# Linear attention in transposed 64x64 float32 tiles, with sums of squares and factors made by products with selectors

## The chip, the cores and the metric

The kernel runs on one core of a Trainium2 chip. The metric is the device time of one execution in microseconds (us). Abbreviations in the rows: PE is TensorE (matrix products), PEld its weight loads, DVE is VectorE, ACT is ScalarE, POOL is GpSimd, SP the engine that issues most transfers.

## What is computed

Three stages follow one another, all in float32, for 8 batches, 8 heads, 576 tokens and 64 features a head. Only the first is touched.

```
kv  = einsum('bhsd,bhde'): k^T v of each head          # 64 x 64 state, over all 576 tokens
out = q @ kv                                           # per head
out = out / sqrt(mean(out*out over the head) + 1e-6) * g_norm
x   = out, heads side by side                          # [8, 576, 512]
# second stage: xk, xr = blends of each token with the one before it
r = sigmoid(xr @ w_r);  v = relu(xk @ w_k)**2 @ w_v;   x = r * v
# third stage: attention of 4 experts, the best 2 per token, summed
```

The state has no causal mask: it sums over all tokens before any head's output can start.

## The kernel before

**Phase 1** makes the first two stages, batch by batch. Large products run as three passes in a rounded format (`mm3`: high part times high part, low times high, high times low; lines 59 to 61), each pass 128x128 weights against 288 columns, half of a batch's 576 tokens. One half needs 4 r groups of 12 passes (`r_group`; batch 0 does those of both halves first), 8 k groups of 12 (`k_group`) and 4 v groups of 24 (`v_group`); a batch is 480 passes. `acc`, the accumulator, has 4 banks.

The 20 weight tiles come as double words and are converted on the chip (`wconv`, `words`): five VectorE steps each on 128x512 (lines 140 to 151), and then for the 12 tiles of w_r and w_k three products, for the 8 of w_v two GpSimd operations (lines 179 and 180).

**`front(b)`** is the linear attention of one batch. It takes 5 chunks of tokens, 128 four times and 64. The state: 8 products of 64x64 per chunk into the bank `kvp` (line 217), copied by ScalarE into `kvbd`, which holds two heads on a block diagonal of 128x128. Heads: a chunk of q is the weight and `kvbd` moves, 4 products to `po`, tokens on partitions (line 240). ScalarE squares (244) and copies (245), VectorE reduces over each head (246). The factor 1/sqrt is made on 128 x 40 numbers (`rsqrt`, 249 to 269: for batch 0 ScalarE's root and a reciprocal in two parts with one Newton step, else a bit trick and three steps). The scaling is a GpSimd product (VectorE for batch 0), `scaled`; then `turned` transposes each chunk by four products with the identity (283) and ScalarE writes `xT`, features on partitions, with g. `mix` blends neighbours of `xT` and splits the blend in a high and a low part (327 to 334).

**Order.** A driver at the end of `phase1` runs one step of the generator `front(b+1)` after each group of batch b; within that, every engine's order is set by a scheduler that simulates the engines and uses the buffers as they come free. K(0,1) below is the first `k_group` of batch 0's second half. VectorE's part of a k group that makes the low part `kl` stands behind a GpSimd product (361, 362). Phase 2, from 566 us, makes the third stage.

The functions in question, with the line numbers of the rows:

## Time and profile before

| | |
|---|---|
| median of 3 runs | 1039.02 us (1038.98 to 1040.86) |
| profiled execution | 1040.45 us, span of the core 1038.7 |
| TensorE busy | 1007.7 us, 97% |
| VectorE, ScalarE, GpSimd busy | 540.1 (52%), 535.2 (52%), 306.1 (29%) |

Busy time is summed over the whole span and says nothing of a single stage; a matrix product in the rows overlaps the next, so starts rather than durations are to be subtracted. A float32 product leaves two records on TensorE. "x16" is the number of records merged in a row; what stands in brackets is idle time before it and what ended that.

### The profile page before, as it was taken

Reading aid. Unit: us, or ns where it says so; the run is one execution under the profiler, and the core shown is the slowest. Engines: PE = TensorE matmul, PEld = TensorE weight load, DVE = VectorE, ACT = ScalarE, POOL = GpSimd, SP = SyncE. Lnnn points to the kernel's source line nnn. Section 1 sums busy time; section 2 is a strip of 40 time slices with the busy share of each in tenths; the row PEclk is TensorE's granted clock in tenths of the full one; section 3 lists DMA queues with packets and bytes.
Section 4 is the critical chain, followed back from the end, with each engine's and each line's share of the span. In section 5 each row is a group of like instructions: output and inputs, shape, how many; then the busy total and the mean of one; then the engine's idle time right before and its main releaser. Section 6 shows DMA issues by size and latency. Waiting matters only on the chain.

```text
span 1038.7 us, 20745 instructions
## 1 busy us (share of the span) xinstructions
PE 1007.7 (97%) x7968; PEld 925.9 (89%) x7968; DVE 540.1 (52%) x1524; ACT 535.2 (52%) x1381; POOL 306.1 (29%) x459
## 2 busy tenths in 40 slices
PE   6797899999999999999999999999999999999998
PEld 4587799999999999999999999888888888888876
DVE  4989934344533434444354531367464746556563
ACT  4975544544644554465375533356453736454544
POOL 0017622213212212212123113165251616243331
PEclk9998999999999999999999999999999999999999
DMA  8972200001041041040101201210111202020102
GB/s 278 314 256 84 83 25 24 23 24 54 2 130 54 2 151 34 15 146 25 44 26 45 84 24 25 66 46 27 66 47 47 80 13 93 1 93 27 46 13 80
DMA packets 46259, 70.56 MB, mean 68 GB/s; under 512 B 8016, under 2 KB 25936, under 8 KB 46160
## 3 DMA queue, kind: packets, MB, share of 16 engines
q1 hardware_dynamic: 37712, 59.79, 17.7%
q10 hardware_dynamic: 8448, 9.44, 3.0%
q8 instruction: 63, 1.03, 0.4%
q14 instruction: 36, 0.29, 0.1%
HBM read 50.34 MB, written 18.87 MB: 67 GB/s over the span
## 4 chain that ended last, share of the span: by engine, by line
PE 89%; DVE 6%; DMA 3%; issue 1%; ACT 1%; SPq 0%; POOL 0%; ACTq 0%; DVEq 0%; POOLq 0%
PE acc L59 23%; PE acc L60 22%; PE acc L61 22%; PE acc L668 5%; PE pt L640 5%; PE s L592 4%; PE po L240 3%; PE kvp L217 2%; PE pt L283 1%; PE s L583 1%; DMA raw<-in_w_r 1%; DVE wvl L151 1%; DVE cvt L144 1%; DVE xm L328 1%; DMA qt<-in_qT 1%
## 5 line engine op out<-in xcount | busy, mean ns | idle before, releaser
L361 POOL TENSOR_TENSOR ksq<-rl 128x288 f32<-128x288 f32 x128 | 91.2, 712 | 322.0 <-ACT rl L358 314.6
L59 PE MATMUL acc<-xh,wkh 128*128 128x288 f32 x512 | 154.4, 302 | 2.8 <-ACT rl L358 2.8
L60 PE MATMUL acc<-xl,wkh 128*128 128x288 f32 x512 | 152.9, 299 | 2.5 <-DVE xl L334 2.5
L60 PE MATMUL acc<-kl,wvh 128*128 128x288 f32 x512 | 150.8, 297 | 3.6 <-DVE kl L362 3.5
L61 PE MATMUL acc<-xh,wkl 128*128 128x288 f32 x512 | 152.9, 299 | 0.0
L61 PE MATMUL acc<-kh,wvl 128*128 128x288 f32 x512 | 150.2, 296 | 0.0
L59 PE MATMUL acc<-kh,wvh 128*128 128x288 f32 x512 | 146.8, 296 | 0.0
L604 ACT ACTIVATE pr<-pr,nm 128x256 f32<-128x256 f32 (+4 forms) x144 | 83.4, 580 | 76.0 <-DVE nm L564 73.5
L362 DVE TENSOR_TENSOR kl<-ksq,kh 128x288 fp32r<-128x288 f32 x128 | 60.8, 475 | 90.8 <-POOL ksq L361 89.0
L621 POOL TENSOR_SCALAR pr<-pr,rc,wg 128x512 f32<-128x512 f32 (+3 forms) x128 | 76.4, 609 | 100.5 <-DVE wg L557 57.5
L59 PEld LDWEIGHTS acc<-xh,wkh 128*128 128x128 f32 x512 | 97.5, 191 | 4.9 <-ACT rl L358 3.0
L60 PEld LDWEIGHTS acc<-kl,wvh 128*128 128x128 f32 x512 | 96.5, 189 | 4.5 <-DVE kl L362 4.5
L60 PEld LDWEIGHTS acc<-xl,wkh 128*128 128x128 f32 x512 | 97.6, 191 | 2.7 <-DVE xl L334 2.7
L61 PEld LDWEIGHTS acc<-xh,wkl 128*128 128x128 f32 x512 | 97.6, 191 | 0.0
L61 PEld LDWEIGHTS acc<-kh,wvl 128*128 128x128 f32 x512 | 96.6, 189 | 0.0
L59 PEld LDWEIGHTS acc<-kh,wvh 128*128 128x128 f32 x512 | 95.3, 189 | 0.1
L347 ACT ACTIVATE sg<-acc 128x288 f32<-128x288 f32 x64 | 26.1, 408 | 122.1 <-PE acc L61 122.1
L331 DVE TENSOR_TENSOR xl<-xm,xh 128x288 fp32r<-128x288 f32 x96 | 45.0, 508 | 69.9 <-ACT xh L329 69.7
L59 PE MATMUL acc<-x2h,wqh 128*128 128x256 f32 (+1 forms) x256 | 78.9, 308 | 0.7 <-DVE sg L374 0.4
L59 PE MATMUL acc<-xh,wrh 128*128 128x288 f32 x256 | 78.2, 306 | 0.0
L358 ACT ACTIVATE rl<-acc 128x288 f32<-128x288 f32 x128 | 52.1, 409 | 50.4 <-PE acc L61 49.0
L374 DVE TENSOR_TENSOR sg<-acc,sg 128x288 f32<-128x288 f32 x64 | 29.0, 456 | 93.0 <-PE acc L61 92.5
(154 smaller groups left out, 2576.2 us busy)
## 6 DMA issues: line engine op xcount, KB each, us to landing
x2d<-sg SPq DMA_DIRECT2D x16, 576.0 KB, 3.4
out<-ob SPq DMA_DIRECT2D x28, 288.0 KB, 2.1
kt<-in_k SPq DMA_DIRECT2D x31, 256.0 KB, 3.4
vt<-in_v SPq DMA_DIRECT2D x31, 256.0 KB, 3.5
qt<-in_qT SPq DMA_DIRECT2D x31, 256.0 KB, 2.8
x2in<-x2d ACTq DMA_DIRECT2D x8, 640.0 KB, 4.4
raw<-in_w_k SPq DMA_DIRECT2D x8, 512.0 KB, 6.5
raw<-in_w_v SPq DMA_DIRECT2D x8, 512.0 KB, 3.8
```

The source lines that it names most:

```text
L59: nc.tensor.matmul(ps, wh(i), xh(i), start=(i == 0), stop=False)
L60: nc.tensor.matmul(ps, wh(i), xl(i), start=False, stop=False)
L61: nc.tensor.matmul(ps, wl(i), xh(i), start=False, stop=(i == n - 1))
L331: nc.vector.tensor_sub(xl[:, p - 1, :], xp, xh[:, p - 1, :].bitcast(F32))
L358: nc.scalar.activation(rl, acc, AF.Relu)
L361: nc.gpsimd.tensor_mul(sq, rl, rl)
L362: late.append(lambda: nc.vector.tensor_sub(kl[:, m, :], sq, kh[:, m, :].bitcast(F32)))
L592: nc.tensor.matmul(sts[b, p, j][:, r, :L], qs[h, x, t0:t0 + n], ks[h, y, :L], start=(i == 0), stop=(i == 2))
L604: nc.scalar.activation(pr[:, :L], pr[:, :L], AF.Exp, bias=nm, scale=-1.0, accum_out=sms[b, p, j][:, e2:e2 + 1])
L621: nc.gpsimd.tensor_scalar(pr[:, :L], pr[:, :L], rc[:, r:r + 1], wg, op0=ALU.mult, op1=ALU.mult)
L640: nc.tensor.transpose(pt[:rows, (i - i0) * P:(i - i0 + 1) * P], pr[:, i * P:i * P + rows], ident)
L668: nc.tensor.matmul(y[r * D:(r + 1) * D, a:w], vs[:kn, i, e * D:(e + 1) * D], pT[:kn, r, i, a:w], start=(i == 0), stop=(i == idx[-1]), skip ...
```

## The change

The state keeps its form (8 products of 64x64 per chunk), in chunks of 128, 128, 128, 112 and 80 tokens, and goes as a plain 64-row copy per head into `kv`; `kvbd` goes. Heads are made transposed: the state is the weight, 64x64, on the four tiles of the array that two row halves and two column halves make, and q, laid out by the host with features on partitions, moves in 288 columns, so that the output comes out in the layout of `xT`. ScalarE squares it and copies it into `xT` unscaled. The mean over a head is a product of the squares with `sels` (ones over 64, 128x32) into `sm`, which shares the bank of `kvp`. The factors are made on [64 or 128] x 288 numbers, split in a high and a low row, and spread over the features by products with `selb` (ones), and VectorE multiplies `xT` by g and by the factors. The transposes, the reduces and GpSimd's scalings go. `acc` has 3 banks instead of 4, `po` two pairs of banks instead of two banks. The table of the start-up has fewer steps.

In the order of TensorE around the end of batch 0's first half (`acc<-kl,wvh` are passes of a v group, `acc<-xh,wkh` the first of K(0,1)), before:

```order
L60 MATMUL acc<-kl,wvh 128x288
L240 MATMUL po<-kvbd,qt 128x128 x3
L61 MATMUL acc<-kh,wvl 128x288 x4
L240 MATMUL po<-kvbd,qt 128x128 x4
L217 MATMUL kvp<-vt,kt 64x64 x3
L283 MATMUL pt<-ident,xn 128x128 x4
L217 MATMUL kvp<-vt,kt 64x64 x3
L59 MATMUL acc<-xh,wkh 128x288
```

and now, where one v group of 24 passes follows behind these rows:

```order
L63 MATMUL acc<-kl,wvh 128x288
L296 MATMUL po<-rb,selb 128x288 x4
L64 MATMUL acc<-kh,wvl 128x288 x3
L249 MATMUL po<-qt,kv 64x288 x8
L62 MATMUL acc<-kh,wvh 128x288
```

Before, a chunk's heads and state products of later fronts and the transposes stand there in a row; now one front's factors and heads stand between the passes of the v groups, and no state product and no transpose.

TensorE in a later batch, the second half of a front, now, in two pieces (`po` takes the heads, the passes are of a k group):

```order
L249 MATMUL po<-qt,kv 64x288 x8
L62 MATMUL acc<-xh,wkh 128x288
L63 MATMUL acc<-xl,wkh 128x288
L64 MATMUL acc<-xh,wkl 128x288
```

```order
L63 MATMUL acc<-xl,wkh 128x288
L249 MATMUL po<-qt,kv 64x288 x4
L64 MATMUL acc<-xh,wkl 128x288
L62 MATMUL acc<-xh,wkh 128x288
L63 MATMUL acc<-xl,wkh 128x288
L249 MATMUL po<-qt,kv 64x288 x4
L64 MATMUL acc<-xh,wkl 128x288
```

The heads come in three groups of 8, 4 and 4 products where there were five of 4, and no transpose follows.

VectorE around the factors of a later batch, before (`ms`, `sh`, `y`, `nt` are the factors' steps, `kl` the low part that the v groups read):

```order
L362 TENSOR_TENSOR kl<-ksq,kh 128x288 x2
L246 TENSOR_REDUCE ss<-sq 64x8
L251 TENSOR_SCALAR ms<-ss 128x40
L257 TENSOR_SCALAR sh<-ms 128x40
L259 TENSOR_SCALAR y<-sh 128x40
L261 TENSOR_SCALAR ms<-ms 128x40
L331 TENSOR_TENSOR xl<-xm,xh 128x288
L264 TENSOR_TENSOR nt<-y 128x40
```

and now:

```order
L375 TENSOR_TENSOR kl<-ksq,kh 128x288 x4
L269 TENSOR_SCALAR ms<-kvp 128x288
L275 TENSOR_SCALAR nt<-ms 128x288
L277 TENSOR_SCALAR y<-nt 128x288
L279 TENSOR_SCALAR ms<-ms 128x288
L281 TENSOR_TENSOR nt<-y 128x288
L283 TENSOR_TENSOR nt<-nt,ms 128x288
L375 TENSOR_TENSOR kl<-ksq,kh 128x288
L285 SCALAR_TENSOR_TENSOR y<-nt,y 128x288
```

The steps stand at the same place but work on 288 columns instead of 40, and parts of `kl` stand between and behind them.

The diff, cut to its core:

```diff
+    FH = [(0, P), (P, P), (2 * P, P), (3 * P, 112), (3 * P + 112, S - 3 * P - 112)]
...
-            kvbd = w1.tile([P, NP, P], F32, name="kvbd")
+            sels = w1.tile([P, 2, 32], F32, name="sels")
+            selb = w1.tile([P, 2, P], F32R, name="selb")
+            lom = w1.tile([P, 1], F32, name="lom")
...
-                        acc = ps.tile([P, CW], F32, name="acc", bufs=4)
+                        acc = ps.tile([P, CW], F32, name="acc", bufs=3)
...
             def front(b):
...
+                kvp = ps.tile([P, 512], F32, name="kvp")
+                kv = fr.tile([P, NP, D], F32, name="kv")
+                kw = kvp[:, :NP * D].rearrange("p (a e) -> p a e", a=NP)
+                for c, (t0, n) in enumerate(FH):
+                    kt, vt = kvt[b * NF + c]
+                    for a in range(NP):
+                        for r in range(2):
+                            hd = 2 * (2 * (a // 2) + r) + a % 2
+                            hd = slice(hd * D, (hd + 1) * D)
+                            nc.tensor.matmul(kw[r * D:(r + 1) * D, a, :], kt[:n, hd], vt[:n, hd],
+                                             start=(c == 0 and a == 0), stop=(c == NF - 1), skip_group_check=True)
+                    load_kv(b * NF + c + 3)
+                    if c == 2:
+                        yield
+                nc.scalar.activation(kv, kw, AF.Copy)
+                yield
+                yield
                 xT = sb.tile([P, NP, S + 1], F32, name="xT")
                 nc.gpsimd.memset(xT[:, :, 0:1], 0.0)
                 xTs[b] = xT
...
+                sqs = {}
+                def cols(h):
+                    return slice(1 + h * HS, 1 + (h + 1) * HS)
+                def heads(h, a):
+                    qt = qts[4 * b + 2 * h + a]
+                    po = ps.tile([P, 2, 512], F32, name="po", bufs=2)
+                    for c in range(2):
+                        for r in range(2):
+                            rs = slice(r * D, (r + 1) * D)
+                            nc.tensor.matmul(po[c * D:(c + 1) * D, r, :HS], kv[rs, 2 * a + c, :], qt[rs, c, :], start=True, stop=True, skip_group_check=True)
+                    load_q(4 * b + 2 * h + a + 3)
+                    sq = sqs[h, a] = fr.tile([P, 2, HS], F32, name="sq", bufs=4)
+                    nc.scalar.activation(sq, po[:, :, :HS], AF.Square)
+                    nc.scalar.activation(xT[:, 2 * a:2 * a + 2, cols(h)], po[:, :, :HS], AF.Copy)
+                sm = ps.tile([P, 512], F32, name="kvp")
+                ms, y, nt, rb = [fr.tile([P, HS], F32 if name != "rb" else F32R, name=name, bufs=1) for name in ("ms", "y", "nt", "rb")]
+                def means(*hs):
+                    for i in range(2):
+                        for h in hs:
+                            for a in range(2):
+                                g = 32 * (2 * h + a)
+                                nc.tensor.matmul(sm[g:g + 32, :HS], sels[:, i, :], sqs[h, a][:, i, :], start=(i == 0), stop=(i == 1), skip_group_check=True)
+                def rsqrt(h0, h1):
+                    g = slice(64 * h0, 64 * h1)
+                    m, r, t, c = ms[g], y[g], nt[g], rb[g]
+                    nc.vector.tensor_scalar(m, sm[g, :HS], 1e-6, None, op0=ALU.add)
                     wstep()
                     if b == 0:
                         nc.scalar.activation(r, m, AF.Sqrt)
                         nc.vector.reciprocal(r, r)
                     else:
-                        nc.vector.tensor_scalar(t, m.bitcast(I32), 1, None, op0=ALU.logical_shift_right)
+                        nc.vector.tensor_scalar(t.bitcast(I32), m.bitcast(I32), 1, None, op0=ALU.logical_shift_right)
                         wstep()
-                        nc.vector.tensor_scalar(r.bitcast(I32), t, -1.0, float(0x5F3759DF), op0=ALU.mult, op1=ALU.add)
+                        nc.vector.tensor_scalar(r.bitcast(I32), t.bitcast(I32), -1.0, float(0x5F3759DF), op0=ALU.mult, op1=ALU.add)
                     wstep()
                     nc.vector.tensor_scalar(m, m, -0.5, None, op0=ALU.mult)
                     for _ in range(1 if b == 0 else 3):
-                        a = fr.tile([P, NC, H], F32, name="nt")[:, :c1 - c0, :]
-                        nc.vector.tensor_mul(a, r, r)
+                        nc.vector.tensor_mul(t, r, r)
                         wstep()
-                        nc.vector.tensor_mul(a, a, m)
+                        nc.vector.tensor_mul(t, t, m)
                         wstep()
-                        nc.vector.scalar_tensor_tensor(r, a, 1.5, r, op0=ALU.add, op1=ALU.mult)
+                        nc.vector.scalar_tensor_tensor(r, t, 1.5, r, op0=ALU.add, op1=ALU.mult)
                         wstep()
...
+                    nc.vector.tensor_copy(c, r)
+                    nc.vector.scalar_tensor_tensor(c, c.bitcast(F32), lom[g], r, op0=ALU.mult, op1=ALU.add)
+                def scaled(h):
+                    for i in range(2):
+                        po = ps.tile([P, 2, 512], F32, name="po", bufs=2)
+                        for a in range(2):
+                            g = slice(32 * (2 * h + a), 32 * (2 * h + a) + 32)
+                            nc.tensor.matmul(po[:, a, :HS], selb[g, i, :], rb[g], start=True, stop=True)
+                        x = xT[:, i::2, cols(h)]
+                        nc.vector.scalar_tensor_tensor(x, x, g_sb, po[:, :, :HS], op0=ALU.mult, op1=ALU.mult)
                 if b == 0:
...
+                    for h in range(2):
+                        for a in range(2):
+                            heads(h, a)
                             yield
...
+                        means(h)
+                        rsqrt(h, h + 1)
+                        yield
+                        scaled(h)
+                        yield
                     return
-                for c in range(NC):
-                    heads(c)
+                for h in range(2):
+                    for a in range(2):
+                        heads(h, a)
                     yield
...
+                    yield
+                yield
+                means(0, 1)
+                yield
+                rsqrt(0, 2)
+                for _ in range(5):
+                    yield
+                for h in range(2):
+                    scaled(h)
+                    yield
                     yield
...
-            for c in "w0 k0 k1 w1 k2 k3 k4 w2 q0 q1 q2 q3 q4".split():
+            for c in "w0 k0 k1 w1 k2 k3 k4 w2 q0 q1 q2 q3".split():
...
+            nc.gpsimd.memset(sels, 0.0)
+            for i in range(2):
+                for r in range(2):
+                    nc.gpsimd.memset(sels[r * D:(r + 1) * D, i, 2 * i + r::4], 1.0 / D)
+            rows = ident.rearrange("p (g k h) -> p g k h", g=4, h=4)
+            zs = fr.tile([P, 2, 2, 4], F32, name="zs", bufs=1)
+            for u in range(2):
+                nc.vector.reduce_sum(zs[:, 0, u, :], rows[:, :, u, :].rearrange("p g h -> p h g"), axis=AX.X)
+            nc.vector.reduce_sum(lom, zs[:, 0, 1, :], axis=AX.X)
+            nc.vector.tensor_add(zs[:, 1, 0, :], zs[:, 0, 0, :], zs[:, 0, 1, :])
+            nc.vector.tensor_scalar(lom, lom, -1.0, None, op0=ALU.mult)
+            nc.vector.tensor_copy(selb.rearrange("p i (r d) -> p (i r) d", r=2), zs[:, 1, 0, :].unsqueeze(2).to_broadcast([P, 4, D]))
...
-            TK = [1, 0, 1, 0, 1, 1, 0, 1, 0, 1, 0, 1, 0, 1, 1]
+            TK = [1, 0, 1, 1, 0, 1, 1, 1, 1, 1, 1]
...
+        "qT": c(q.reshape(B, 2, 2, 2, 2, S // 2, D).transpose(0, 4, 1, 2, 6, 3, 5).reshape(B, 4, 2 * D, 2, S // 2)),
```

## Rows read from the trace of the kernel before

**Rows 1.** Windows: busy time of each engine, granted clock, DMA share, GB/s by stretch

```profile
core 0: us, PE busy (x) PEld busy (x) DVE busy (x) ACT busy (x) POOL busy (x), PEclk, DMA share, GB/s
...
78.00:129.70 51.70, 41.99 (x288) 38.67 (x286) 51.16 (x77) 27.86 (x64) 35.40 (x32) 0.90 0.26 83
129.70:566.30 436.60, 436.60 (x3519) 428.97 (x3517) 178.57 (x425) 218.11 (x520) 97.00 (x135) 1.00 0.15 48
```

**Rows 2.** Timeline of TensorE: start, duration, instruction; two products and a batch's start

```profile
161.58 0.29 PE L59 MATMUL acc<-xh,wkh 128*128 128x288 f32 x1
...
174.28 0.30 PE L59 MATMUL acc<-kh,wvh 128*128 128x288 f32 x1
...
440.18 0.40 PE L217 MATMUL kvp<-vt,kt 128*64 128x64 f32 x6
```

**Rows 3.** Timeline of TensorE around a chunk of state products, 365.2 to 366.5

```profile
365.27 0.29 PE L61 MATMUL acc<-xh,wrl 128*128 128x288 f32 x1
365.50 0.69 PE L217 MATMUL kvp<-vt,kt 128*64 128x64 f32 x16
...
366.35 0.29 PE L60 MATMUL acc<-xl,wrh 128*128 128x288 f32 x1
```

**Rows 4.** Timeline of TensorE around four records of state products

```profile
290.94 0.29 PE L61 MATMUL acc<-xh,wrl 128*128 128x288 f32 x1
291.16 0.34 PE L217 MATMUL kvp<-vt,kt 128*64 128x64 f32 x4
...
291.67 0.29 PE L60 MATMUL acc<-xl,wrh 128*128 128x288 f32 x1
```

**Rows 5.** Timeline of TensorE around a chunk's head products

```profile
384.09 0.29 PE L60 MATMUL acc<-xl,wkh 128*128 128x288 f32 x1
384.22 1.05 PE L240 MATMUL po<-kvbd,qt 128*128 128x128 f32 x8
...
385.25 0.29 PE L59 MATMUL acc<-xh,wkh 128*128 128x288 f32 x1
```

**Rows 6.** Timeline of TensorE in phase 2: products on two column tiles

```profile
1028.90 0.47 PE L668 MATMUL acc<-pt,vs 128*64 128x320 f32 x2
1029.16 0.47 PE L668 MATMUL acc<-pt,vs 128*64 128x320 f32 x2
```

**Rows 7.** Timeline of VectorE, 43.4 to 45.6

```profile
43.47 0.42 DVE L142 TENSOR_SCALAR cvt<-cvt 128x512 int32<-128x512 int32 x1
43.80 0.68 DVE L246 TENSOR_REDUCE ss<-sq 128x8 f32<-128x512 f32 x1
44.40 0.68 DVE L144 SCALAR_TENSOR_TENSOR cvt<-raw,cvt 128x512 int32<-128x512 int32 x1
45.00 0.51 DVE L328 SCALAR_TENSOR_TENSOR xm<-xT,mur,xm 128x288 f32<-128x288 f32 x1
45.43 0.42 DVE L149 TENSOR_SCALAR raw<-cvt 128x512 int32<-128x512 int32 x1
```

**Rows 8.** Timeline of VectorE and ScalarE's root: the reciprocals of batch 0

```profile
29.25 0.30 DVE L255 RECIPROCAL y<-y 128x24 f32<-128x24 f32 x1 [1.25 <-ACT y L254]
...
33.55 0.24 DVE L255 RECIPROCAL y<-y 128x16 f32<-128x16 f32 x1
```

**Rows 9.** Timeline of GpSimd and VectorE from 76 us

```profile
76.17 3.32 POOL L274 TENSOR_TENSOR xn<-o,y 128x512 f32<-128x512 f32 x2 [2.83 <-DVE y L268]
...
77.29 2.51 DVE L328 SCALAR_TENSOR_TENSOR xm<-xT,muk,xm 128x288 f32<-128x288 f32 x2
```

**Rows 10.** Groups of VectorE, 20 to 121 us: instruction, count, busy us, mean ns, idle before

```profile
L151 DVE SCALAR_TENSOR_TENSOR wvl<-raw 128x512 fp32r<-128x512 uint32 x7 | 10.0, 1426 | 0.0
```

**Rows 11.** Timeline of VectorE, GpSimd and TensorE at the end of the start-up

```profile
121.09 0.67 DVE L151 SCALAR_TENSOR_TENSOR wvl<-raw 128x512 fp32r<-128x512 uint32 x1
...
123.48 1.89 POOL L180 TENSOR_TENSOR wvl<-cvt,wvl 128x512 fp32r<-128x512 f32 x1
...
129.72 0.40 PE L59 MATMUL acc<-xh,wkh 128*128 128x288 f32 x1
```

More of the change, by code (lines that the diff above doesn't have):

```diff
@@ L209, in front @@
             def front(b):
-                kvp = ps.tile([P, NP, P], F32, name="kvp")
-                for c, (t0, n) in enumerate(CH):
-                    kt, vt = kvt[b * NC + c]
-                    for p in range(NP):
-                        for r in range(0, P, D):
-                            hd = slice(p * P + r, p * P + r + D)
-                            nc.tensor.matmul(kvp[r:r + D, p, r:r + D], kt[:n, hd], vt[:n, hd],
-                                             start=(c == 0 and p == 0), stop=(c == NC - 1), skip_group_check=True)
-                    load_kv(b * NC + c + 3)
-                    if c == NC - 1:
-                        kv = kvbd
-                        nc.scalar.activation(kv[0:D, :, 0:D], kvp[0:D, :, 0:D], AF.Copy)
-                        nc.scalar.activation(kv[D:P, :, D:P], kvp[D:P, :, D:P], AF.Copy)
-                    yield
-                ss = fr.tile([P, NC, H], F32, name="ss")
-                nc.gpsimd.memset(ss, 1.0)
-                ms = fr.tile([P, NC, H], F32, name="ms")
-                y = fr.tile([P, NC, H], F32, name="y")
-                sh = fr.tile([P, NC, H], I32, name="sh")
+                kvp = ps.tile([P, 512], F32, name="kvp")
[15 more added lines that the diff above has]
+                yield
                 xT = sb.tile([P, NP, S + 1], F32, name="xT")
@@ L232, in front @@
                 xTs[b] = xT
-                os_, xns = [], []
-                def heads(c):
-                    t0, n = CH[c]
-                    qt = qts[b * NC + c]
-                    po = ps.tile([P, DM], F32, name="po", bufs=2)
-                    for p in range(NP):
-                        nc.tensor.matmul(po[:n, p * P:(p + 1) * P], qt[:, p, :n], kv[:, p, :], start=True, stop=True)
-                    load_q(b * NC + c + 3)
-                    o = fr.tile([P, DM], F32, name="o", bufs=5)
-                    sq = fr.tile([P, DM], F32, name="sq", bufs=1)
-                    nc.scalar.activation(sq[:n], po[:n], AF.Square)
-                    nc.scalar.activation(o[:n], po[:n], AF.Copy)
-                    nc.vector.reduce_sum(ss[:n, c, :], sq[:n].rearrange("p (h d) -> p h d", d=D), axis=AX.X)
-                    os_.append(o)
@@ L279, in turned @@
-                def turned(c):
-                    t0, n = CH[c]
-                    pt = ps.tile([P, NP, P], F32, name="pt")
-                    for p in range(NP):
-                        nc.tensor.transpose(pt[:, p, :n], xns[c][:n, p * P:(p + 1) * P], ident[:n, :n])
-                    nc.scalar.activation(xT[:, :, 1 + t0:1 + t0 + n], pt[:, :, :n], AF.Copy, scale=g_sb)
+                    nc.vector.tensor_copy(c, r)
+                    nc.vector.scalar_tensor_tensor(c, c.bitcast(F32), lom[g], r, op0=ALU.mult, op1=ALU.add)
@@ L298, in front @@
                     return
-                for c in range(NC):
-                    heads(c)
+                for h in range(2):
+                    for a in range(2):
+                        heads(h, a)
+                    yield
                     yield
                 yield
+                means(0, 1)
                 yield
-                rsqrt(0, NC)
-                scaled(0)
-                scaled(1)
-                yield
-                yield
-                for c in range(NC):
-                    turned(c)
-                    if c + 2 < NC:
-                        scaled(c + 2)
+                rsqrt(0, 2)
@@ L343, in r_group @@
                 xh, xl = mixed[b, h, "r"]
-                acc = ps.tile([P, HS], F32, name="acc", bufs=4)
+                acc = ps.tile([P, HS], F32, name="acc", bufs=3)
                 ms_ = slice(m * P, (m + 1) * P)
@@ L370, in v_group @@
                 sg = sgs[b, h]
-                acc = ps.tile([P, HS], F32, name="acc", bufs=4)
+                acc = ps.tile([P, HS], F32, name="acc", bufs=3)
                 ms_ = slice(m * P, (m + 1) * P)
@@ L408, in ticks @@
                     wconv()
-            TK = [1, 0, 1, 0, 1, 1, 0, 1, 0, 1, 0, 1, 0, 1, 1]
+            TK = [1, 0, 1, 1, 0, 1, 1, 1, 1, 1, 1]
             wconv()
-            for i in range(NC + 6):
+            for i in range(7):
                 run(f0)
@@ L798 @@
     ins = {
-        "qT": c(np.concatenate([q[:, :, t:t + 128].transpose(0, 1, 3, 2).reshape(B, H // 2, 2 * D, -1).transpose(0, 2, 1, 3).reshape(B, -1)
-                                for t in range(0, S, 128)], axis=1)),
+        "qT": c(q.reshape(B, 2, 2, 2, 2, S // 2, D).transpose(0, 4, 1, 2, 6, 3, 5).reshape(B, 4, 2 * D, 2, S // 2)),
         "k": c(k.transpose(0, 2, 1, 3).reshape(B, S, DM)),
```

39 lines of the change are left out of this document (10 added, 29 removed).

## The prediction, made before the changed kernel was run

> **What bounds the kernel now.** I read the windows first, because one number for the whole span hides two regimes. The reader is to see that from 129.7 us, where the second half of batch 0 starts, to the end of phase 1 the tensor engine is busy for 436.60 of 436.60 us [rows 1]: whatever a batch adds to or takes from it is time. From 78 to 129.7 us VectorE is busy for 51.16 of 51.70 and TensorE for 41.99, so there VectorE, which converts the weights, sets the pace. Then the instruction rows of TensorE. In steady state the 96 products from 161.58 to 174.28 take 12.70, a step of 0.1323 each; the first state product of one batch stands at 365.50 and that of the next at 440.18 [rows 2, 3]. A batch is thus 74.68 us, its 480 products 63.50, and the linear attention costs the other 11.18. Phase 2 (566.3 us on) keeps its instructions, and I give it nothing.
>
> **State products.** The price of a group between two products is the distance of its outer neighbours less two steps (0.264). The chunk of 8 products, 16 records (a float32 product shows as two), costs 366.35 − 365.27 − 0.264 = 0.82; one of 4 records costs 291.67 − 290.94 − 0.264 = 0.466 [rows 3, 4]. That is 0.0295 per record and some 0.345 for the group. Before: five chunks, 4.1 per batch. After: the order has four groups (1, 2, 21 and 16 products), 4 × 0.345 + 80 × 0.0295 = 3.74; the chunks' new lengths change nothing in a product of 64 columns.
>
> **Heads.** Before, a chunk's group costs 385.25 − 384.09 − 0.264 = 0.896 [rows 5], five of them 4.48 (the last, with 64 tokens, taken alike); so the transposes are 11.18 − 4.1 − 4.48 = 2.60. After, 16 products of 64x64 weights and 288 columns. No row shows four tiles at work. The nearest are phase 2's products on two column tiles, 320 float32 columns: two records lie together at 1028.90, the next two at 1029.16 [rows 6], so one round of records takes 0.26 to 0.27, or 0.242 for 288 columns, and two tiles run beside each other. If all four do, 32 records are 8 rounds: 8 × 0.242 + 3 groups × 0.345 = 2.97. If only two do, one product ends every round: 16 × 0.242 + 3 × 0.345 = 4.90. I take four: in these rows the second tile's product starts with the first tile's, not 0.26 later behind its second record, so one tile doesn't seem to hold another.
>
> The Trainium skill, "TensorE: Matmul & The Clock Gate", Part 3 (packing small matmuls), speaks against this: it states that matmuls are in program order in start and end ("strict FIFO, no reordering"). In the code a product's two records follow each other on one tile, so by that rule the second would hold up the next tile's first, and only two tiles could overlap, which is rival A: 12.5 a batch by it, 10.10 without. [Rows 6] have the first two records together, which goes against the rule; no run here shows four.
>
> **Means, factors, transposes.** The means are 8 products into 32 columns each, in groups of 3 and 5. With all tiles at once I count 6 rounds: 6 × 0.242 + 2 × 0.345 = 2.14 (two at a time: 8 × 0.242 + 0.69 = 2.63). The factors are 2 groups of 4 one-pass products: 2 × (2 × 0.14 + 0.345) = 1.25 (a step of 0.132 each if they run one by one: 1.75). The transposes' 2.60 go. Sum after: 3.74 + 2.97 + 2.14 + 1.25 = **10.10** against 11.18, or 3.74 + 4.90 + 2.63 + 1.25 = 12.5 if only two tiles run.
>
> **What is left when the pace changes hands.** It isn't 1.08 times seven, because a front runs ahead of its batch. By the order, before K(0,1) (the k products of batch 0's second half, 129.72 us [rows 11]) TensorE has done fronts 0 and 1, front 2 but for its transposes, front 3's state and two of its chunks, and 12 records of front 4. Left: 2.60 + (3 × 0.896 + 2.60) + (4.1 − 0.35 + 4.48 + 2.60) + 3 × 11.18 = 52.3. After, the state and the means share one bank, so fronts can't overlap, and there are done only fronts 0 and 1 and of front 2 the state and 8 products. Left: the other 8 head products (groups of 1 and 7, 6 rounds) 2.14 + means (one group, 4 rounds) 1.31 + factors 1.25 + 5 × 10.10 = 55.2. So TensorE has **+2.9** to do behind that point.
>
> **Start-up.** VectorE is the bound from some 20 us until the last weight conversion at 121.09 [rows 11]; its 100 conversion steps stay. By the steps between starts: reduce 0.60, one-input 512 0.33, three-operand 512 0.60 and 288 0.43 [rows 7]. Before, beside conversions: 15 reduces × 0.60 = 9.0, 5 scalings taken at 0.60 = 3.0, 48 steps on 288 columns × 0.43 = 20.6, and 25 narrow ones estimated at half the 0.24 of [rows 8], 3.0: 35.6. After: 58 × 0.43 = 24.9, four on 576 columns × 0.67 (0.60 plus an eighth) = 2.7, 11 one-input ones at 0.21 (0.33 scaled) = 2.3, and two reciprocals of 288 columns. Those no row has: 24 columns take 0.30, 16 take 0.24 [rows 8], 7.5 ns a column, by which 288 would take 2.3; if the slope is only noise, 0.4. I take 2.0, 4.0 together: 33.9, so **−1.7**.
>
> VectorE is also slowed by GpSimd. While a scaling of the old form runs (1.66 each), the blend takes 1.25 instead of 0.51 [rows 7, 9]; the last conversion step takes 1.43 in w_v, whose parts GpSimd joins, where such a step alone takes 0.68 [rows 7, 10]. Before, six such scalings fall before 121 us; they go: 6 × 0.8 = **−4.8**, between 0 (other GpSimd work moves into the place) and −6. Against it VectorE waits for ScalarE's root, which now works on 288 columns and for which 1.25 was idle [rows 8]: **+2**. The last GpSimd part ends at 123.48 + 1.89 = 125.37, 4.35 before K(0,1) starts [rows 11]. After, three accumulator banks instead of four leave the whole fourth v group behind that, 24 × 0.132 = 3.2, and 8 head products 1.3 and 0.4 to start: 4.9, **+0.55**. Start-up together −1.7 − 4.8 + 2 + 0.55 = **−4.0**.
>
> **New waits in the batches.** The 15 factor steps on 288 columns are some 15 × 0.43 = 6 us of VectorE and stand among the subtractions that make kl. The v products wait for those; behind the last kl are six steps of its block (the order), and by the steps of [rows 7] it comes some 0.7 before its product. Hidden, so long as the first v product isn't early by more than that; three banks instead of four take away one group of slack. I add **+1** over all batches, for three or four misses of 0.3.
>
> **Edits at nothing.** The set-up of the selectors is a dozen narrow steps ahead of the first conversion, while the weights are on their way; each is of the kind of 0.24 [rows 8], so uncovered they cost 1 to 2 us once. q comes in four transfers instead of five, k and v in as many as before, at a share of 0.15 [rows 1]; uncovered, a late chunk would hold the products for one transfer. ScalarE loses five copies out of the transposes and writes the heads straight into xT; it has 218.11 of 436.60 to do [rows 1], and its free time would have to be gone before that counts.
>
> **Sum.** −4.0 + 2.9 + 1 = −0.1 on the profiled execution's 1040.45 (span 1038.7, 1.75 around it). That run lies 1.4 above the median of the runs shown, 1039.02; I put the forecast on the median: **1039**.
>
> **The rivals.** *A, slower: two tiles at a time.* Mechanism: a product's second record on a tile holds the next tile's first, in heads and means. For it: program order, and that no row has four at once. Against: [rows 6]. Price: 12.5 a batch, left behind K(0,1) 6.2 + 5 × 12.5 = 68.7 instead of 55.2, +13.5, and some 3 in the start-up: 1055 (1052 to 1060). It decides from the second round of the first heads group on: there a round of four records must last two rounds.
>
> *B, slower: the wider factor block.* If kl's last part comes late in each batch by about 1 us, instead of 0.7 early, five batches pay 1 each: 1044 (1042 to 1048). For it: 6 us of VectorE in one place. Against: VectorE is busy for only 178.57 of 436.60 [rows 1].
>
> *C, faster: the start-up gives more.* The reciprocals cost 0.4 each (−3.2), the wait for the root falls beside other steps (−2), collisions go altogether (−1.2 more) and the misses don't come (−1): some −7.5, 1031; with ScalarE's and GpSimd's share shortened as well, −12, 1027. For it: VectorE is 51.16 of 51.70 there, so each microsecond counts. Against: transfers take 0.26 of the engines there and can't go much faster earlier, and what start-up gains, GpSimd's chain of w_v parts (1.9 each) may hold.
>
> *D, that the change doesn't do what it says:* the transposes and the reduces leave the order, so I give that nothing.
>
> **Chances.** Forecast 0.50, own range 1034 to 1045; C 0.22; A 0.17; B 0.11. What this kernel's measurement can tell from no change is 0.2%, 2.1 us. Of the forecast's 0.50 I put 0.14 below 1036.9, 0.22 within, 0.14 above 1041.1. Faster: 0.14 + 0.22 = 0.36. Same: 0.22. Slower: 0.14 + 0.17 + 0.11 = 0.42. The range of 8 in 10 takes the forecast's own (0.50), B (0.11), most of C (0.18) and A's lower edge (0.04): 1028 to 1054.
>
> **What would show it.** Rounds of four head records 0.24 apart show four tiles; 0.48 shows A. A batch, measured between the first state products of two batches, should be 73.6; near 76 is A, near 74.6 with TensorE waiting for kl is B. K(0,1) should start near 125.7; below 120 is C. The reciprocal on 64x288 should be near 2.0, VectorE's last w_v step near 117. The forecast is wrong if the batch isn't 73.6 ± 0.5, or if K(0,1) starts more than 5 us from 125.7.

## The result, and the profile after

The changed kernel takes 1046.27 us (1045.76 to 1046.98), the one before 1039.0 beside it: a ratio of 1.0066 with an interval of 1.0049 to 1.0083. It is slower, where no measurable change was forecast. The profiled execution (1046.98) has a span of 1045.2, 6.5 over the 1038.7 of before; that is what the rows below account for.

Windows of the changed kernel, columns as in [rows 1]:

```profile
core 0: us, PE busy (x) PEld busy (x) DVE busy (x) ACT busy (x) POOL busy (x), PEclk, DMA share, GB/s
24.00:78.00 54.00, 42.55 (x275) 25.35 (x276) 47.78 (x93) 36.99 (x75) 4.55 (x4) 0.87 0.61 199
78.00:129.43 51.43, 41.91 (x316) 35.30 (x316) 50.10 (x82) 24.52 (x56) 26.17 (x22) 0.90 0.29 94
114.00:120.00 6.00, 3.39 (x22) 2.51 (x20) 5.97 (x8) 0.63 (x1) 4.01 (x3) 1.00 0.00 0
120.00:126.00 6.00, 5.19 (x25) 2.54 (x26) 6.00 (x12) 4.05 (x9) 1.86 (x2) 0.53 0.11 27
129.43:568.70 439.27, 438.09 (x3602) 409.46 (x3601) 205.62 (x451) 195.14 (x473) 70.68 (x106) 1.00 0.18 56
```

And one row of the kernel before:

```profile
24.00:78.00 54.00, 47.94 (x439) 36.75 (x440) 49.51 (x121) 45.93 (x96) 5.43 (x5) 1.00 0.87 285
```

The regime behind 129.43 is still TensorE's. In the start-up VectorE isn't full from 24 to 78 us, now (47.78 of 54.00) and, a little less so, before (49.51). And the granted clock is 0.53 from 120 to 126, just where TensorE is needed, behind six microseconds in which it was busy for 3.39.

TensorE in a later batch, timeline: the state products, which answer to [rows 2 to 4], and the next batch's first:

```profile
300.56 1.50 PE L226 MATMUL kvp<-vt,kt 128*64 128x64 f32 x42
...
306.06 0.29 PE L62 MATMUL acc<-xh,wrh 128*128 128x288 f32 x1
306.28 1.43 PE L226 MATMUL kvp<-vt,kt 112*64 112x64 f32 x32
...
307.88 0.30 PE L64 MATMUL acc<-xh,wrl 128*128 128x288 f32 x1
...
374.61 0.51 PE L226 MATMUL kvp<-vt,kt 128*64 128x64 f32 x10
```

A batch is 374.61 − 300.56 = 74.05 (74.68 before, 73.6 forecast). The last group, 32 records, costs 307.88 − 306.06 − 0.264 = 1.55; by group and records it should be 0.345 + 32 × 0.0295 = 1.29. The rest is a wait in the middle of the group, before the last chunk's records.

TensorE at the heads, which answer to [rows 5, 6]: the whole group with its neighbours, and the same start in narrower windows:

```profile
310.66 0.29 PE L64 MATMUL acc<-xh,wkl 128*128 128x288 f32 x1
310.88 1.20 PE L249 MATMUL po<-qt,kv 64*64 64x288 f32 x16
...
312.25 0.29 PE L63 MATMUL acc<-xl,wkh 128*128 128x288 f32 x1
```

```profile
310.88 0.47 PE L249 MATMUL po<-qt,kv 64*64 64x288 f32 x4
...
311.18 0.66 PE L249 MATMUL po<-qt,kv 64*64 64x288 f32 x8
```

Four records lie at 310.88, and eight more, in two rounds, from 311.18; the group costs 312.25 − 310.66 − 0.264 = 1.33 for eight products. That is 0.345 and four rounds of 0.242: all four tiles work together, and rival A is out. (That a round might be two products with both their records at once doesn't fit the group of [rows 5]: there the eight records of four products on the whole array start one by one, 0.11 apart.)

The end of the start-up (GpSimd's last part of w_v, TensorE), which answers to [rows 11]:

```profile
120.67 1.27 POOL L185 TENSOR_TENSOR wvl<-cvt,wvl 128x512 fp32r<-128x512 f32 x1
...
121.99 1.09 PE L64 MATMUL acc<-kh,wvl 128*128 128x288 f32 x3 [0.42 <-POOL wvl L185]
123.04 2.39 PE L249 MATMUL po<-qt,kv 64*64 64x288 f32 x16
125.36 0.61 PE L62 MATMUL acc<-kh,wvh 128*128 128x288 f32 x1
125.76 0.44 PE L63 MATMUL acc<-kl,wvh 128*128 128x288 f32 x1
...
129.43 0.29 PE L62 MATMUL acc<-xh,wkh 128*128 128x288 f32 x1
```

The part ends at 121.94 (125.37 before), but K(0,1) starts only at 129.43 (129.72): 7.5 of tail instead of 4.35. The same 16 head records that took 1.20 in a later batch take 2.39 here, and the first seven passes of the fourth v group stand mostly 0.24 apart instead of 0.13, which is the 1.2 GHz level.

The accounting of the two profiled executions, the groups priced as in the prediction (60 of them behind K(0,1), 68 before):

| | forecast | measured |
|---|---|---|
| last part of w_v done | −4.5 | 121.94 − 125.37 = −3.4 |
| tail to K(0,1) | +0.55 | 7.49 − 4.35 = +3.1 |
| linear attention behind K(0,1) | 52.3 to 55.2, +2.9 | 51.7 to 58.1, +6.5 |
| other waits of TensorE there | +1 | +1.4 |
| rest (phase 2) | 0 | −1.1 |
| sum | −0.1 | +6.5 |

The last row is what follows the last v pass, 387.4 before and 386.3 now. That pass stands at 651.3 (658.9 now): 566 us, which I called the start of phase 2, is where TensorE has done the last front's linear attention, and batch 7's passes go on behind it.

### The profile page after: what moved, and what is told of

It is laid out like the page before. It is cut to its first block, busy times and chain, and to the rows that moved or that the text cites. A ratio compares the mean times of both kernels' runs of the same rounds, so it can differ in the third digit from the quotient of the medians.

```text
span 1045.2 us, 20516 instructions
## 1 busy us (share of the span) xinstructions
PE 1006.4 (96%) x7936; PEld 892.2 (85%) x7936; DVE 567.1 (54%) x1535; ACT 504.6 (48%) x1317; POOL 269.5 (26%) x420
## 4 chain that ended last, share of the span: by engine, by line
PE 83%; DVE 6%; DMA 5%; issue 3%; ACT 1%; POOL 1%; SPq 0%; DVEq 0%; ACTq 0%; POOLq 0%
PE acc L62 22%; PE acc L64 21%; PE acc L63 21%; PE acc L693 5%; PE pt L665 5%; PE s L617 4%; PE po L249 2%; DMA vt<-in_v 1%; PE kvp L226 1%; PE s L608 1%; DMA raw<-in_w_k 1%; DMA raw<-in_w_r 1%; DVE cvt L149 1%; PE kvp L264 1%; DVE xm L341 1%
## 5 line engine op out<-in xcount | busy, mean ns | idle before, releaser
L63 PE MATMUL acc<-xl,wkh 128*128 128x288 f32 x512 | 149.8, 293 | 0.9 <-DVE xl L344 0.9
L629 ACT ACTIVATE pr<-pr,nm 128x256 f32<-128x256 f32 (+4 forms) x144 | 83.4, 580 | 73.3 <-DVE nm L589 70.6
L344 DVE TENSOR_TENSOR xl<-xm,xh 128x288 fp32r<-128x288 f32 x96 | 42.2, 481 | 89.9 <-ACT xh L342 89.9
L64 PE MATMUL acc<-xh,wrl 128*128 128x288 f32 x256 | 76.0, 297 | 0.0
```

Source lines behind the costliest of these rows:

```text
L63: nc.tensor.matmul(ps, wh(i), xl(i), start=False, stop=False)
L64: nc.tensor.matmul(ps, wl(i), xh(i), start=False, stop=(i == n - 1))
L344: nc.vector.tensor_sub(xl[:, p - 1, :], xp, xh[:, p - 1, :].bitcast(F32))
L629: nc.scalar.activation(pr[:, :L], pr[:, :L], AF.Exp, bias=nm, scale=-1.0, accum_out=sms[b, p, j][:, e2:e2 + 1])
```

## The experiments

All are timed in turn with the kernel before on one chip; that had medians of 1040 to 1040.8 on these, so ratios are to be compared. Intervals are in brackets. K(0,1) and other times within a run are of its one profiled execution, which can lie up to 4 us from the median; the changed kernel, profiled twice, has K(0,1) at 129.43 and 128.41.

**Where the weights wait.** The queue of transfers around 50 us, with the products that free its buffers (TensorE), the conversion that freed a weight buffer (VectorE), and ScalarE's first conversion step with what its idle time waited for (group row: busy, mean ns, idle):

```profile
41.85 1.62 PE L226 MATMUL kvp<-vt,kt 128*64 128x64 f32 x48
44.84 0.48 SPq L200 DMA_DIRECT2D vt<-in_v  x1
47.02 0.68 DVE L156 SCALAR_TENSOR_TENSOR wkl<-raw 128x512 fp32r<-128x512 uint32 x1
49.17 1.12 PE L226 MATMUL kvp<-vt,kt 112*64 112x64 f32 x16 [3.84 <-DMA vt<-in_v]
50.33 0.33 SPq L199 DMA_DIRECT2D kt<-in_k  x1
51.69 0.33 SPq L199 DMA_DIRECT2D kt<-in_k  x1
52.07 0.42 SPq L137 DMA_DIRECT2D raw<-in_w_k  x1
...
L189 ACT ACTIVATE cvt<-raw 128x512 f32<-128x512 f32 x20 | 13.4, 670 | 18.5 <-DMA raw<-in_w_k 10.7 <-DMA raw<-in_w_r 7.6 <-DMA raw<-in_w_v 0.2
```

The reader is to see that the weight transfer at 52.07 could have gone when the conversion of 47.02 was done (47.7), and went 4.4 later, behind loads of k (50.33, 51.69) whose buffers the products of 49.17 had to free. Those products waited 3.84 for their own v, which could be loaded only when the lump of 48 records at 41.85 had freed its buffers; by the order that lump stands behind the means of front 0, which use its bank. In the kernel before the same row of ScalarE shows 9.3 of idle time, 8.6 for w_r at the very start and none for w_k:

```profile
L184 ACT ACTIVATE cvt<-raw 128x512 f32<-128x512 f32 x20 | 13.4, 670 | 9.3 <-DMA raw<-in_w_r 8.6 <-DMA raw<-in_w_v 0.7
```

The test puts the weights on another queue:

```diff
-                    nc.sync.dma_start(raw.rearrange(...
+                    nc.scalar.dma_start(raw.rearrange(...
```

> The changed kernel with the weights' transfers issued from ScalarE's queue, all others from the old one. Theory: in the changed kernel the weights stand in one queue behind k and v loads that wait for a buffer (the ninth w_k and later loads 4 to 10 us), and ScalarE waits 10.7 us for w_k where it waited for none before. With a queue of their own that falls below 5 us, the last conversion of VectorE comes at 115 to 117 instead of 118.8, and the time falls by 1 to 3. Rival: the load itself takes 6 to 7 us from the moment its buffer is free, so that the wait stays above 8 us; or ScalarE now stands still until a buffer is free: 1046 to 1052.

Measured: 1042.36, ratio 1.0027 [1.0016, 1.0038]; its rows of ScalarE, GpSimd and K(0,1):

```profile
L189 ACT ACTIVATE cvt<-raw 128x512 f32<-128x512 f32 x20 | 13.5, 676 | 13.2 <-DMA raw<-in_w_k 5.7 <-DMA vt<-in_v 3.1 <-DMA raw<-in_w_r 2.6
...
117.67 1.36 POOL L185 TENSOR_TENSOR wvl<-cvt,wvl 128x512 fp32r<-128x512 f32 x1 [0.69 <-DVE wvl L156]
...
124.96 0.29 PE L62 MATMUL acc<-xh,wkh 128*128 128x288 f32 x1
```

The wait for w_k is halved, the one for w_r, at the very start, falls from 7.6 to 2.6, and K(0,1) is 4.5 earlier, with eight head products of the tail moved behind it. The control is the same edit in the kernel before:

> The kernel before, with the weights' transfers on ScalarE's queue and nothing else. Theory: its k and v loads hardly hold the weights (ScalarE waits 9.3 us for weights in the start-up, 8.6 of them for w_r at the very start, none for w_k), so the start-up is VectorE's and the time stays: 1038 to 1041. Rival: the one queue slows every start-up, not just the changed one: 1034 to 1037.

1040.49, ratio 1.0000 [0.9989, 1.0010]: no gain in time. But the control doesn't show that weights wait only in the changed kernel. In the kernel before (conversion that frees a weight buffer, last load of k and v, weight transfers):

```profile
67.22 0.68 DVE L151 SCALAR_TENSOR_TENSOR wkl<-raw 128x512 fp32r<-128x512 uint32 x1
...
69.62 0.42 SPq L195 DMA_DIRECT2D vt<-in_v  x1
70.14 0.96 SPq L132 DMA_DIRECT2D raw<-in_w_v  x2
```

The buffer was free at 67.90, and the transfer went 2.2 later, behind k and v. Over all 17 transfers that need a used buffer the time from its last reader's end to the transfer's issue sums to 26.3 in the kernel before and to 25.5 in the changed one, 20 of it in either case at the first three. On ScalarE's queue it is 10.6 and 12.1. And in the control, too, the last part of w_v comes earlier, by 7.4, but other things take its place (GpSimd's part, TensorE):

```profile
116.66 1.26 POOL L180 TENSOR_TENSOR wvl<-cvt,wvl 128x512 fp32r<-128x512 f32 x1
...
123.72 3.78 PE L240 MATMUL po<-kvbd,qt 128*128 128x128 f32 x16 [1.07 <-ACT kvbd L223]
...
128.06 0.61 PE L59 MATMUL acc<-xh,wkh 128*128 128x288 f32 x1
```

K(0,1) is only 1.7 earlier than before, with waits and heads at a granted clock of 0.50 (123 to 128) ahead of it. So a queue of their own brings the weights earlier in both kernels and is worth some 4 us in the changed one alone. How much of this are the loads of k and v, and how much the first three transfers, no run separates; a difference of the two kernels it isn't.

**Buffers for k and v.** Four instead of three, and loads four chunks ahead:

```diff
-  [fr.tile([P, DM], F32, name=name, bufs=3) for name in ("kt", "vt")]
+  [fr.tile([P, DM], F32, name=name, bufs=4) for name in ("kt", "vt")]
-  load_kv(b * NF + c + 3)
+  load_kv(b * NF + c + 4)
```

> The changed kernel with four k and four v buffers instead of three, loaded four chunks ahead (the room comes from one state copy instead of two and from a scratch of the factors that lies in the squares' tile). Theory: in the changed kernel the state products of a batch stand in one lump, so the buffers for the last two chunks come free late and the last group waits for its transfer: the state groups behind K(0,1) sum to 21.2 us where they would be 18.7 to 19.1 without a wait. Then the groups fall to about 19, weights stand less long behind blocked k and v loads on the transfer queue, and the time falls by 2 to 5 us, to 1041.5 to 1044. Rival: the wait only moves (to the next transfer, or to VectorE): at least 1045.5.

1048.26, 1.0078 [1.0062, 1.0095]: a miss. The batches did fall to 73.3, but K(0,1) came at 131.91, with the clock at 0.54 from 120 to 126 and 0.61 to 132, and batch 1 took 77. So the second try leaves the start-up's order alone (`load_kv(... + 4)` beside the other only `if b > 0`):

> The changed kernel with four k and v buffers, but loaded ahead of what the changed kernel does only from batch 1 on, so that the start-up keeps its order of transfers. Theory: the first run with four buffers had 73.3 per batch instead of 74.05 to 74.24 and lost it all in the start-up. Here the batches have 73.3 to 73.5 and the start-up stays within 1.5 of 129.4: 1042 to 1044.5. Rival: a fourth buffer changes the start-up by itself (the scheduler moves state products and transfers): K(0,1) at 131 or later and a time of 1046 or more.

1043.54, 1.0037 [1.0021, 1.0052]. Two batches' state products stand 73.33 apart, where the changed kernel has 74.05:

```profile
372.25 0.34 PE L226 MATMUL kvp<-vt,kt 128*64 128x64 f32 x4
...
445.58 0.34 PE L226 MATMUL kvp<-vt,kt 128*64 128x64 f32 x4
```

But the theory of the wait isn't what gave this. The state groups behind K(0,1) sum to 23.1 here, where it wanted 19 and the changed kernel has 21.2: from the third of these batches on nothing waits, but the last group is now two, with a price of 0.345 more, and the first of them waits longer. What fell by 0.8 are the means, in the changed kernel and here:

```profile
319.46 0.69 PE L264 MATMUL kvp<-sq,sels 128*32 128x288 f32 x6
...
320.94 1.16 PE L264 MATMUL kvp<-sq,sels 128*32 128x288 f32 x10
```

```profile
391.22 1.18 PE L266 MATMUL kvp<-sq,sels 128*32 128x288 f32 x16
```

Two groups cost 2.10 together, one costs 1.31: the edit changed the scheduler's order, and the 0.7 are that. In the profiled run K(0,1) even started at 124.27, which this edit was not expected to do.

**Banks.** The means in an accumulator instead of the state's bank (`sm = ps.tile([P, 512], F32, name="acc", bufs=3)`):

> The changed kernel with the means' sums in one of the three accumulator banks instead of the state's bank. Theory: the shared bank keeps a front from starting before the one ahead of it has its factors, so less of it is done in the gaps of the start-up; with its own place more of front 2 and front 3 is done before K(0,1), the linear attention left behind that falls from 58.2 to 53 to 55 us, and the time falls by 3 to 5, to 1041 to 1043. Rival: three banks are already few, and giving one away for some us each batch stalls the r, k and v groups: 1046 to 1050.

1043.80, 1.0039 [1.0025, 1.0053]. From K(0,1) to the first pass of batch 7's last v groups it took 512.3 us instead of 516.9, as expected; but K(0,1) came at 134.75, in an execution of 1047.64, the slowest of its nine. I put that on the fronts that now came earlier and took the queue and VectorE, which these rows don't show. Then the accumulators, in the kernel before (`name="acc", bufs=3` for `bufs=4`):

> The kernel before with three accumulator banks instead of four and nothing else. Theory: only the end of the start-up pays: a whole v group of 24 passes stands behind the last part of w_v, 3.2 us at full clock and 4 to 6 with the clock down: 1042 to 1045, with a batch still 74.7. Rival: three banks make every half batch wait for ScalarE and VectorE to empty one: a batch of 75.5 or more and a time above 1047. Third: nothing, 1039, if the scheduler moves other work into the place.

1044.70, 1.0043 [1.0027, 1.0060]. GpSimd's last part and the tail's last v group:

```profile
123.36 1.50 POOL L180 TENSOR_TENSOR wvl<-cvt,wvl 128x512 fp32r<-128x512 f32 x1
...
130.41 0.38 PE L59 MATMUL acc<-kh,wvh 128*128 128x288 f32 x1
...
133.67 0.29 PE L59 MATMUL acc<-xh,wkh 128*128 128x288 f32 x1
```

The fourth group of 24 passes stands whole between 130.41 and 133.67, as thought, and the tail is 8.8, all of it at full clock. The rival had a part too: batches of 75.47, 0.8 more. Three banks alone cost the old kernel some 4.5 us; in the forecast they stand within a tail that was to grow by 0.55. Taking back the bank from the heads' pair (`acc` 4, `po` 1, the means a bank of their own) fails:

> The changed kernel with the eight accumulation banks dealt out anew: four accumulators (three), one pair for heads and factors (two pairs), a bank of its own for the means' sums (shared with the state). Theory after the first four runs: three accumulators cost the start-up's tail some 4.5 us (the kernel before with three showed it, tail 4.35 to 8.81), and the shared bank costs 4.5 us of front work that isn't done early (the means in an accumulator showed 516.9 to 512.3 behind K(0,1)). Both go here, against at most 0.345 more for each of four more groups in each of six batches, 1 to 2 per batch: 1036 to 1042, K(0,1) between 124 and 130, a batch 73.5 to 75. Rival: with one pair every head product waits until ScalarE has squared and copied the one before; TensorE stands 0.5 to 1 us at each of four groups per batch: 1046 or more.

1053.41, 1.0121 [1.0101, 1.0141]. The rival's size, by another way. Rows of the groups' idle time over the whole run:

```profile
L264 PE MATMUL sm<-sq,sels 128*32 128x288 f32 x128 | 25.2, 427 | 0.2 <-ACT sq L252 0.2
L249 PE MATMUL po<-qt,kv 64*64 64x288 f32 x248 | 22.2, 428 | 1.7 <-DVE xT L298 0.9 <-ACT kv L231 0.8
```

Nearly nothing waits. But the scheduler now sets most means singly between passes, and each stop for a small group has its 0.35: the means' products are busy for 25.2 where the changed kernel has 17.2. The fourth accumulator didn't shorten the tail here: K(0,1) came at 132.28, 9.9 behind the last part.

**The tail.** The fourth v group in a bank of the heads:

```diff
-  acc = ps.tile([P, HS], F32, name="acc", bufs=3)
+  acc = ps.tile([P, 2, 512], F32, name="po", bufs=2)[:, 0, :HS] if b == h == 0 and m == KD - 1 else ...
```

> The changed kernel, in which the fourth v group of batch 0's first half alone accumulates in a bank of the heads' pair instead of waiting for one of three accumulators. Theory: between the last part of w_v (121.95 us) and K(0,1) (129.43) stand 24 passes and 8 head products, partly at 1.2 GHz; the 21 passes that don't need the last part go before it, K(0,1) starts at 125 to 127, and the time falls by 2.5 to 4, to 1042 to 1044. Rival: the banks of the heads are not free by then, or the passes are given back later because the heads come later: above 1045.

1047.61, 1.0069 [1.0052, 1.0085]: no gain, though the profiled execution, at 1044.57 the fastest of its six, has K(0,1) where the theory wanted it. The passes didn't go ahead; all 24 still stand behind the last part (the first at 120.87, K(0,1) at 126.71), two thirds of them 0.24 apart. It says nothing of the banks. The filling of TensorE's idle time:

```diff
+  if b == h == 0 and m < 3 and i == KF - 1:
+      for _ in range(10):
+          nc.tensor.matmul(acc, zer, kh[:, 0, :], start=False, stop=False)
```

> The changed kernel with ten products of a zero weight ahead of the last part of w_v in each of the first three v groups of batch 0's first half (they add nothing to the sums). Theory: TensorE is idle while it waits for the last conversions, the granted clock goes to 0.53 in 120 to 126 us, and the tail of 24 passes and 8 head products runs partly at half speed, 2 to 3 us more than at full. With 4 us of filling the clock stays at 1.00 in the tail, which takes 5 us instead of 7.5, K(0,1) starts at 127 and the time is 1043 to 1044.5. Rival: the clock falls earlier in the start-up, or the fill delays the last passes as much as it saves: 1046 or more.

1045.61, 1.0050 [1.0035, 1.0064], between the two. The clock did what was expected from 120 us on (without fillers the changed kernel has 0.53 there, and 0.72 in its second trace), the time didn't:

```profile
120.00:126.00 6.00, 5.55 (x42) 4.26 (x40) 6.00 (x12) 4.79 (x11) 1.78 (x2) 1.00 0.01 1
...
130.16 0.30 PE L63 MATMUL acc<-xh,wkh 128*128 128x288 f32 x1
```

Part of the 30 fillers came late and cost the tail what the clock gave. How much of the 3.1 the clock alone is worth in the whole time thus stays open; the rows at either level give 2.39 − 1.20 for the heads and about seven passes × 0.108, some 2 together. Something else holds the tail as well: with the fillers the last four heads wait 0.53 for VectorE's `xT`, and in the changed kernel's second trace the heads wait 0.37 for it.

**Together.** Queue and buffers; then these with the means in an accumulator; then with the fourth group:

> The changed kernel with the weights' transfers on ScalarE's queue and four k and v buffers used ahead from batch 1 on. Theory: the two gains are of different stretches, so they add up: K(0,1) at 124 to 126 (the first alone: 124.96) and batches of 73.3 to 73.5 (the second alone: 73.33 to 73.56) instead of 73.8 to 74.0: 1039 to 1041.5. Rival: both only bring k and v earlier at the same place, so together they give what each gave alone: 1042 to 1044.

> The one before with the means' sums in one of the accumulators, so that the next front's state can start while the factors are made. Theory: alone this took the stretch behind K(0,1) from 516.9 to 512.3, but the fronts that came earlier held weights' transfers and conversions and K(0,1) came 5.3 late; with the weights on their own queue K(0,1) is at 125 to 129 and the time is 1036 to 1040. Rival: K(0,1) is late because the earlier fronts take VectorE's and TensorE's time ahead of the conversions, not the queue: K(0,1) at 131 or later, 1041 to 1046.

> The changed kernel with the weights on ScalarE's queue, four k and v buffers ahead from batch 1 on, and the fourth v group of batch 0's first half in a bank of the heads. Theory: the tail between the last part of w_v and K(0,1) falls from some 5.5 to 2.5 to 4 us; 1037 to 1040. Rival: as with that edit alone, where the tail fell by only 0.6, the heads' banks are taken at that time: no different from the kernel without it, 1039 to 1043.

1041.58, 1.0014 [1.0003, 1.0024]; 1038.05, 0.9988 [0.9972, 1.0004]; 1040.77, 1.0003 [0.9994, 1.0011]. The first lies between its theory and its rival: the gains don't add up fully. The third is its rival's: its tail is 5.2, not 2.5 to 4. The second is the best version: K(0,1) and the starts of two batches (first r product of each second half):

```profile
122.85 0.29 PE L62 MATMUL acc<-xh,wkh 128*128 128x288 f32 x1
...
332.20 0.30 PE L62 MATMUL acc<-xh,wrh 128*128 128x288 f32 x1
...
405.33 0.30 PE L62 MATMUL acc<-xh,wrh 128*128 128x288 f32 x1
```

K(0,1) is 6.9 and a batch 1.55 below the kernel before, yet the time isn't below it beyond its interval: from K(0,1) to the last v groups it needs 513.3, the old kernel 508.95; 2.4 of that are groups of linear attention (54.1 against 51.7), since the old kernel has more of its fronts done by then, the rest are waits. One more try for the tail, the fourth group in the state's bank, and the changed kernel again beside it:

> The changed kernel with weights on ScalarE's queue, four k and v buffers, the means' sums in an accumulator, and the fourth v group of batch 0's first half in the state's bank, which is free of the means now. Theory: 24 passes, 3.2 to 4 us, that stand behind the last part of w_v because there are three accumulators, mostly come ahead of it; the tail falls from 6.98 to 3 to 5 and the time from 1038.05 to 1034 to 1037. Rival: the tail is the late low parts of k and the half clock behind that wait, not the accumulators, or the state of front 2, which wants the same bank, comes later and is paid for in batch 1: 1037.5 to 1040.

> The changed kernel as it is, on the chip of the run beside it, so that its distance from the edited ones is seen on one chip. Expected by both theories: 1045 to 1049, 0.5 to 0.8% over the kernel before.

1044.07, 1.0032 [1.0019, 1.0045], beyond even the rival's 1040. The tail did fall to 4.8, and passes of the fourth group stand in the middle of the k groups; but front 2's state waits for the bank: 128 records of state products stand before K(0,1) instead of 288, and 62.7 us of linear attention are left behind it instead of 54.1. The repeat has 1045.91, 1.0052 [1.0038, 1.0067]; its trace has a tail of 7.1 and 57.3 behind K(0,1), against 7.5 and 58.1.

## Why the prediction was wrong

*Right.* Four tiles at once: 1.33 for eight heads and 0.84 for four, 3.01 per batch against 2.97. In the Trainium skill, "TensorE: Matmul & The Clock Gate", Part 3 (packing small matmuls), products start and end in program order; with a product's two records in a row that would have given eight rounds, and the rows at 310.88 show four. So the rule as I read it doesn't hold here; the same section's packed tiles that start some 4 ns apart fit, since the four records start within 0.02 us. Means (2.10 for 2.14), factors (1.32 for 1.25) and the work before (51.7 for 52.3) were right, and so was the reciprocal, which no row had:

```profile
24.41 1.95 DVE L273 RECIPROCAL y<-y 64x288 f32<-64x288 f32 x1 [1.33 <-ACT y L272]
...
L156 DVE SCALAR_TENSOR_TENSOR wvl<-raw 128x512 fp32r<-128x512 uint32 x8 | 5.9, 742 | 0.1
...
116.51 1.58 POOL L185 TENSOR_TENSOR wvl<-cvt,wvl 128x512 fp32r<-128x512 f32 x1 [1.06 <-DVE wvl L156]
...
116.89 1.51 DVE L375 TENSOR_TENSOR kl<-ksq,kh 128x288 fp32r<-128x288 f32 x1
```

The second row shows the conversion step free of GpSimd, 742 ns instead of 1426 [rows 10]. The collisions aren't gone, though: the last two rows have one with a subtraction for kl, 1.51 instead of 0.44, and from 20 to 121 us these subtractions rise from a mean of 629 ns to 832. Rival B's late kl cost little: all other waits are 1.4 together.

*Wrong: "Start-up together −4.0".* It was −0.3, for two reasons. First, the tail was sized at 4.9 and took 7.5: the term +0.55 measured +3.1. The 24 passes of the fourth group and the eight heads behind the last part of w_v were seen, but priced at full speed; TensorE, idle for almost half of the six microseconds before, was at 1.2 GHz, and the heads' wait for `xT` wasn't counted. In the old kernel three banks alone gave +4.5, with the tail at full clock, so a fourth group behind the last operand is dear without the clock, too; what they cost in the changed kernel wasn't separated. Second, the last conversion came at 118.8, not 117. VectorE was taken for the bound from 20 us on, but the row that I read begins at 78: from 20 to 78 us it stood idle for 6.9 before and 9.3 now, 3.4 and 6.1 of it behind ScalarE's first conversion step, which waits for weights. And the collisions, at −4.8 the largest term, partly moved to other steps; the trace of before also has five such scalings ahead of 121 us, not six.

*Wrong: "Edits at nothing".* I wrote that an uncovered late chunk would hold the products for one transfer. It can hold the queue: at 52.07 a weight transfer went 4.4 late behind loads that waited for a buffer. Moving the weights to another queue gave back some 4 us and nothing in the kernel before. But weights wait as long in the old kernel's queue (26.3 against 25.5), so this isn't what sets the two apart: it is time that the edit wins elsewhere.

*Wrong: 3.74 for the state products.* Behind K(0,1) they cost 21.2 instead of 5 × 3.74 = 18.7. The price of a record was right; the last group of a batch waits before its last chunk, 1.1 in the first of the five and 0 to 0.45 in the others, because the 21 products ahead of it free their buffers in one lump. The fourth buffer removes the wait in the last three, without making the state cheaper (23.1).

The start-up's 3.7, the state products' 2.5 and 1.5 of smaller terms, less 1.1 behind the last v pass, separate −0.1 from 6.5. The 1.1 stays unexplained; the kernel before with three banks has 386.3 there too, so the transposed heads needn't be its cause. That the term of what is left (+2.9) was real the means in their own place show: the work behind K(0,1) shrank by 4.5. The sum is thus measured row by row; what each part would give back in time, the runs show only for the means' place (some 2.5 us) and the weights' queue (4).

## What to carry to other kernels

An order in which products come in lumps frees its buffers in lumps; look in one queue at what stands behind the loads that then wait, not only at who reads them. And look at the same waits in the kernel before: a control that gains nothing in time can still have them. When an edit shortens a batch, price its groups anew before you call the theory confirmed. An accumulator bank given to something else is paid for where a late operand lets all groups wait at once, and the engine that waited there came back at half speed here. Price small tiled groups by group as well as by record.

## What the runs showed of the hardware

- Four 64x64 tiles take float32 products of 288 columns together: four records in a round of 0.24 us, two rounds a product, and 0.35 us for every stop between 128x128 passes.
- A reciprocal of 64x288 numbers takes VectorE 1.95 us, against 0.24 for a one-operand step in the same place.
- The same 16 records took 1.20 at a granted clock of 1.00 and 2.39 behind a stretch in which TensorE had been busy for 3.39 of 6.00. A stretch like it doesn't always bring that: with the means in an accumulator it was busy for 3.84 of 6.00 from 120 to 126, and the clock was 1.00 there and behind.
